# Sums of exp(phi) from a block of ones in the key products, a reordered plan, and 74 unread matmuls in the head

## The chip, the cores and the metric

The kernel runs on one core of a Trainium2 chip. The metric is the device time of one execution in microseconds. The core has a matrix engine (TensorE, PE in the profile; its weight loads are PEld), a vector engine (VectorE, DVE), a scalar engine (ScalarE, ACT), a general engine that here mostly issues loads (GpSimd, POOL) and a queue that issues stores (SyncE, SP). Sixteen DMA engines move data between HBM and the core's memory (SBUF); matmul results go to eight banks of a second memory (PSUM).

## The reference

Attention through 32 memory slots for 8 batches and 8 heads, then a channel mix over the joined heads. Shapes: q, k, v are 8 x 8 x 576 x 64, phi is 8 x 8 x 576 x 32; the weights w_k, w_v, w_r are 512 x 1024, 1024 x 512 and 512 x 512.

```
a = exp(phi - max);  a = a / (sum a + 1e-09)        # max and sum over the 576 tokens
k_m = einsum('bhsm,bhsd->bhmd', a, k);  v_m likewise from v
scores = q @ k_m.T / 8;  attn = softmax(scores)
x = attn @ v_m, heads joined to 512 columns
x_prev = x moved down by one token
xk = mu_k*x + (1-mu_k)*x_prev;  xr = mu_r*x + (1-mu_r)*x_prev
out = sigmoid(xr @ w_r) * (relu(xk @ w_k)**2 @ w_v)
```

What the kernel computes stands to this as follows: it takes exp(phi) without the maximum, multiplies it with k and v, and divides the products afterwards by a sum of exp(phi). The sum runs over the tokens for each head and slot, as the products do; the tile `rz` holds its reciprocal, one column for each of two groups of heads.

## The kernel before

**Tiles.** A token of a batch stands on a partition: the 576 tokens of a head are 64 partitions with nine tokens each (NJ = 9), and 128 partitions hold two heads' worth; four pairs (HH = 4) make a batch. `kvs` are two tiles (one for even, one for odd batches) with room for k and v; `qs` and `ems` (exp(phi) in bf16) are doubled likewise. The channel mix works in c blocks of tokens: block c0 is batch 0 (576 tokens, in halves a of 320 and b of 256 columns), c1 to c8 follow at 512 tokens (448 for the last).

**Order.** There is no loop that sets the order. `PLAN` is a list of words, and the program issues each word's instructions in that order; each engine then runs its own instructions strictly in that order. `BANKS` lists which PSUM bank each new product takes. A word is `batch:step`, `p:load`, `c<block>:<eighth>`, `g:<tile>` or `o:<tile>`.

**Steps of attention** (batch in front of the colon): `exp` (ScalarE, L252) makes exp(phi), `exp0` and `exp1` half of it. `k`, `v`, `kv` (L264) are the products of exp(phi) with k, v or both: 72 matmuls, weights 64 x 32, 64 columns for each of k and v; `k0c` and `k1c` do one half of the rows. `z` (L273) is nine matmuls of exp(phi) with a two-column tile of ones, and a reciprocal on VectorE (L276). `nk` and `ak` (VectorE or ScalarE, L287 for the latter) scale k by it into `kbd`; `nv`, `av` scale v. `tk`, `ta` transpose `kbd` (L321) and copy it (VectorE or ScalarE, L326). `q0`, `q1` turn q on VectorE (L339). `s`, `s0`, `s1` are the scores (32 matmuls, L354) and their exp on ScalarE (L359). The sum over slots and its spreading goes over VectorE (`fe`, `fs`, `fo`, or in smaller parts `qe`, `qs`, `qo`: L386, L396, L398, L405) or, in batch 0, over TensorE and ScalarE for one half (`l0`, `l1`: L369, L374; `h0z`, `h1z`: L379). `y0` to `y3` weigh (L414, tile `atn`). `x0m`, `x1m` are attn @ v_m (L308) and casts on VectorE and ScalarE (L426). `d0d`, `d2d` difference to the previous token (L438), `k0d`, `k0e`, `r0d` and so on mix (L449 to L452) into `xkT` and `xrT`.

**Batch 0** has a shorter way: `nk0`, `nk1`, `nr0`, `nr1` scale v_m by the sums and the mix factors (VectorE, L460, tile `vm`, which reads `mu_m`), and `mk0`, `mk1`, `mr0`, `mr1` (L308, casts L477) give the mixed halves at once. `mub` (L218, with `sel`) makes `mu_m`, `mu` the factors `mu1`.

**Channel mix.** `c1:5` is an eighth of the hidden columns for block 1: four matmuls (L560), relu on ScalarE (L564), square on VectorE (L572), or on ScalarE if the word ends in s (L570). `g:7` is the gate of a 128-token tile (four matmuls L593, tanh L596). `o:7` is its output: eight matmuls (L610), one VectorE instruction (L612) and the store; `o:0a`, `o:0b` are halves of the columns.

**Unread matmuls.** `0:busy4x4` issues four matmuls of a tile of zeros with 4 x 128 columns into a bank that nothing reads (L211).

**Loads.** `p:` words and two before the plan (`PRE`: half of k for batch 0, the identity) are issued on POOL in plan order, except phi of batch 0 (ScalarE's queue) and the mix factors (SP's). In the trace POOL issues a load when the one eight places earlier has landed, or when its buffer is free.

Of the kernel before, what the change touches and what calls it, by code (L numbers as in the profile page):

```python
# [46 lines left out]
    "01234567012345670123407516234075163240567132045671324671035246710352467103254671032546713205467130254671"  # L47
    "30254617302517302465710243657102436571024635170246351760351724603571260547312643712643710524637105247610"
    "5324761053621053612536012534760125346710254736102574631025746310257463102574631025746310257463102574"
# [3 lines left out]
NJ = 9  # L53
# [6 lines left out]
def kernel(  # L60
# [44 lines left out]
    kvs = [const.tile([128, 2, HH, NJ, D], BF16, name=f"kv{i}") for i in range(2)]  # L105
# [16 lines left out]
    def load_rows(dst, src):  # L122
        nc.gpsimd.dma_start(out=dst.rearrange("p h j d -> p h (j d)"), in_=rows(src))  # L123
# [7 lines left out]
    def load_batch(b):  # L131
        for what in LOADS.get(b, LOADS[None]):
            if what == "phi":
                load_phi(b, nc.gpsimd)
            elif what == "q":
                load_q(b)
            else:
                load_rows(kvs[b % 2][:, "kv".index(what)], (k, v)["kv".index(what)][b])

    load_phi(0, nc.scalar)  # L140
    nc.vector.memset(zeros, 0.0)
    mu2 = const.tile([2 * ND, 128], F32, name="mu2")
# [13 lines left out]
    def preload(word):  # L156
# [8 lines left out]
        else:  # L165
# [3 lines left out]
            else:  # L169
                dst = qs[n % 2].rearrange("p (h j) d -> p h j d", j=NJ) if what == "q" else kvs[n % 2][:, "kv".index(what)]  # L170
# [20 lines left out]
    sel = const.tile([2 * ND, 2 * HH, M], F32, name="sel")  # L191
# [7 lines left out]
    mu_m = const.tile([128, 2, 2, 2, D], F32, name="mu_m")  # L199
# [35 lines left out]
    def attention(b):  # L235
# [13 lines left out]
        kv5, em = kvs[b % 2], ems[b % 2]  # L249
# [4 lines left out]
        def ekv(parts, cs=(0, 1)):  # L254

            def go():
                w = parts.stop - parts.start
                kvps = {c: ps_tile([128, w, D], F32, "kvps") for c in cs}
                for i in range(w):
                    st.setdefault("kv"[parts.start + i], {}).update({c: kvps[c][:, i, :] for c in cs})  # L260
# [410 lines left out]
```

## Time and profile before

| | us |
|---|---|
| three timed runs | 203.2, 203.49, 205.34 (median 203.49) |
| the profiled execution | 202.35 |
| its span in the trace | 200.3 |
| its mean granted TensorE clock | 0.996 of full speed |

Rows of a timeline read: start in us, duration in us, engine, line, operation, output<-inputs, shapes, count; the bracket is how long the engine was idle before and what it waited for. Rows that the view has merged give the time from the first start to the last end; the time from one row's start to the next one's is what a step cost its engine. A matmul's row holds its latency too, so two neighbouring rows overlap. The page's columns by stretches give busy us and, in brackets, the count of instructions.

### The profile page before, as it was taken

The numbers are of one execution on the slowest core, as the hardware profiler recorded it, in microseconds if no ns is written. First come the engines' busy times: TensorE is split into PE (matmuls) and PEld (weight loads), VectorE is DVE, ScalarE is ACT, GpSimd is POOL, SyncE is SP. The second block draws the span as 40 slices with busy tenths as digits, with TensorE's granted clock in tenths as the row PEclk, the third lists the DMA queues.
The fourth block names the chain that finished last, engine by engine and source line by source line (L and its number), as shares of the span: only waits on it lengthen the run. The fifth ranks groups of instructions, "written<-read, shape, count | busy, mean of one in ns | idle before, by whom it ended". The sixth has DMA issues, their size and how long they took to land.

```text
span 200.3 us, 5430 instructions
## 1 busy us (share of the span) xinstructions
PE 187.6 (94%) x2186; PEld 98.3 (49%) x2186; DVE 149.3 (75%) x383; ACT 145.3 (73%) x313; POOL 29.8 (15%) x45
## 2 busy tenths in 40 slices
PE   1678999998999999999999999999999999999992
PEld 1355764764554445544456644444444444444451
DVE  2348579999889999999799989999769941132232
ACT  2337999568787899799899987996598679761300
POOL 7843232202123002050300000000000000000000
PEclk9999999999999999999999999999999999999998
DMA  6999999999999999999999202502170060022455
GB/s 161 194 265 209 206 207 253 210 225 289 240 206 285 293 255 202 266 161 271 229 226 218 57 23 65 126 0 56 40 171 2 3 157 0 0 52 55 105 123 139
DMA packets 24522, 31.29 MB, mean 156 GB/s; under 512 B 1961, under 2 KB 19633, under 8 KB 24497
## 3 DMA queue, kind: packets, MB, share of 16 engines
q0 software_dynamic: 17392, 20.91, 55.9%
q1 hardware_dynamic: 6336, 9.18, 17.9%
q10 hardware_dynamic: 768, 0.85, 1.4%
q8 instruction: 17, 0.28, 0.5%
q14 instruction: 9, 0.07, 0.1%
HBM read 38.28 MB, written 9.44 MB: 238 GB/s over the span
## 4 chain that ended last, share of the span: by engine, by line
PE 77%; DMA 17%; POOL 2%; ACT 1%; DVE 1%; issue 1%; POOLq 0%
PE pk L560 29%; PE pv L610 28%; PE pr L593 14%; DMA kv<-in_v_dram 11%; DMA ph<-in_phi_dram 5%; PE kvps L264 3%; PE nops L308 2%; PE scps L354 1%; POOL q L178 1%; POOL kv L126 1%; PE zps L273 1%; ACT em L252 1%; PE mxps L308 1%; DVE atn L414 0%; POOL kv L123 0%
## 5 line engine op out<-in xcount | busy, mean ns | idle before, releaser
L560 PE MATMUL pk<-xkT,wk 128*128 128x512 bf16 (+4 forms) x352 | 68.1, 341 | 0.2 <-ACT xkT L477 0.2
L610 PE MATMUL pv<-wv,sq 128*128 128x512 bf16 (+1 forms) x328 | 66.1, 353 | 0.0
L564 ACT ACTIVATE rl<-pk 128x512 bf16<-128x512 f32 (+3 forms) x80 | 43.5, 553 | 9.9 <-PE pk L560 9.1
L560 PEld LDWEIGHTS <-wk 128*128 128x128 bf16 x352 | 32.8, 98 | 28.7 <-issue 1.0
L610 PEld LDWEIGHTS <-sq 128*128 128x128 bf16 x328 | 31.5, 98 | 29.8 <-issue 0.2
L612 DVE SCALAR_TENSOR_TENSOR o<-sg,pv 128x512 f32<-128x512 f32 (+1 forms) x41 | 24.7, 612 | 15.7 <-PE pv L610 15.2
L593 PE MATMUL pr<-wr,xrT 128*128 128x512 bf16 x144 | 36.1, 380 | 0.2 <-DVE eT L386 0.2
L596 ACT ACTIVATE sg<-pr 128x512 f32<-128x512 f32 x36 | 21.0, 596 | 9.8 <-PE pr L593 9.7
L572 DVE TENSOR_TENSOR sq<-rl 128x320 bf16<-128x320 bf16 (+5 forms) x55 | 16.5, 326 | 15.5 <-ACT rl L564 15.2
L570 ACT ACTIVATE sq<-rl 128x512 bf16<-128x512 bf16 (+5 forms) x49 | 23.7, 504 | 1.2
L449 ACT ACTIVATE mu_d<-diff,mu 128x576 bf16<-128x576 bf16 x26 | 18.7, 774 | 3.8 <-DVE diff L439 2.2
L593 PEld LDWEIGHTS <-xrT 128*128 128x128 bf16 x144 | 13.3, 98 | 15.8 <-issue 0.7
L339 DVE STREAM_TRANSPOSE qT<-q 128x576 uint32<-128x576 uint32 x16 | 11.9, 760 | 4.2 <-DMA q<-in_q_dram 4.2
L426 ACT CAST x<-nops 128x320 bf16<-128x320 f32 (+1 forms) x34 | 11.7, 409 | 4.7 <-PE nops L308 4.6
L414 DVE TENSOR_TENSOR atn<-e,lz 128x256 bf16<-128x256 bf16 (+2 forms) x30 | 12.9, 462 | 0.4 <-ACT lz L379 0.3
L359 ACT ACTIVATE e<-scps 128x288 bf16<-128x288 f32 x32 | 10.5, 416 | 3.5 <-PE scps L354 3.3
L438 DVE TENSOR_TENSOR diff<-x 128x512 bf16<-128x512 bf16 (+1 forms) x42 | 12.3, 349 | 0.6 <-ACT x L426 0.5
L264 PE MATMUL kvps<-kv,em 64*32 64x64 bf16 (+1 forms) x792 | 9.7, 214 | 2.6 <-DMA kv<-in_v_dram 2.0
L264 PEld LDWEIGHTS <-em 64*32 64x32 bf16 x792 | 8.0, 94 | 7.2 <-issue 4.6
L405 DVE STREAM_TRANSPOSE lz<-se 128x576 f32<-128x576 f32 (+3 forms) x17 | 11.4, 686 | 0.0
L452 DVE TENSOR_TENSOR xkT<-x,mu_d 128x1152 bf16<-128x1152 bf16 x14 | 10.4, 752 | 1.4 <-ACT mu_d L449 1.1
L252 ACT ACTIVATE em<-ph 128x1152 bf16<-128x1152 f32 (+1 forms) x9 | 9.3, 1049 | 2.9 <-DMA ph<-in_phi_dram 2.9
(65 smaller groups left out, 147.7 us busy)
## 6 DMA issues: line engine op xcount, KB each, us to landing
out_dram<-o SPq DMA_DIRECT2D x61, 128.0 KB, 2.4
kv<-in_v_dram POOLq DMA_DIRECT2D x8, 576.0 KB, 18.4
ph<-in_phi_dram POOLq DMA_DIRECT2D x7, 576.0 KB, 14.8
kv<-in_k_dram POOLq DMA_DIRECT2D x7, 576.0 KB, 16.8
q<-in_q_dram POOLq DMA_DIRECT2D x6, 576.0 KB, 14.0
q<-in_q_dram POOLq DMA_DIRECT2D x4, 288.0 KB, 12.2
out_dram<-o SPq DMA_DIRECT2D x18, 64.0 KB, 6.1
wk<-in_moe_w_k_dram POOLq DMA_DIRECT2D x2, 512.0 KB, 13.7
```

Source lines behind the costliest of these rows:

```text
L264: nc.tensor.matmul(kvps[c][g * M:(g + 1) * M], lhsT=em[ROWS[c], j, g, :], rhs=kv5[ROWS[c], parts, g, j, :], start=j == 0, stop=j == NJ - 1 ...
L414: nc.vector.tensor_mul(st["at"][:, c, sl], st["e"][:, c, sl], st["lz"][:, c, sl])
L438: nc.vector.tensor_sub(d[:, :, lo:hi], x[:, :, lo:hi], x[:, :, p0:p0 + hi - lo])
L449: nc.scalar.activation(t[:, i], st["d"][:, pr + i, :], AF.Copy, scale=mu1[:, o:o + 1])
L560: nc.tensor.matmul(pk[:, p0 - lo:p1 - lo], lhsT=wk_sb[:, di, fi * 128:(fi + 1) * 128], rhs=xk_T[:, di, p0 % RING:p0 % RING + p1 - p0], sta ...
L564: nc.scalar.activation(rl, pk, AF.Relu, scale=HALF_ROOT)
L570: nc.scalar.activation(sq[:, fi, p:p + p1 - p0], rl[:, part], AF.Square)
L572: nc.vector.tensor_mul(sq[:, fi, p:p + p1 - p0], rl[:, part], rl[:, part])
L593: nc.tensor.matmul(pr, lhsT=xr_T[:, di, c0:c0 + 128], rhs=wr_sb[:, di, :], start=(di == 0), stop=(di == ND - 1))
L596: nc.scalar.activation(gated[t], pr, AF.Tanh, scale=0.5)
L610: nc.tensor.matmul(pv[:, cols], lhsT=sq[:, fi, p:p + 128], rhs=wv_sb[:, fi, cols], start=(fi == 0), stop=(fi == NF - 1))
L612: nc.vector.scalar_tensor_tensor(o[:, cols], in0=gated[t][:, cols], scalar=1.0, in1=pv[:, cols], op0=AL.add, op1=AL.mult)
```

## The change

- `kvs` becomes one tile with five blocks: k of even and odd batches, a block of ones written once by a memset, v of odd and even batches. The steps `ko` and `kov` are the products with k and ones, or k, ones and v: as many matmuls as `k` and `kv`, with 128 and 192 columns in place of 64 and 128. Every column of the ones' product holds the sum, and `zk` (or `zk0`, `zk1` for one half) takes its first column's reciprocal for each half: two VectorE instructions. Batches 1 to 7 use them and have no `z` step; batch 0 keeps `z`, now between `k0c` and `k1c`.
- `sel` and `mu_m` take the memory of two later work tiles (the fourth of `sg` and of `o`).
- The unread matmuls become 23 of 512 columns, 16 of 384, 25 of 128 and 10 of 256 (74), in place of 4, 3, 7, 1 and 12 (27).
- `PLAN` and `BANKS` are written anew throughout. At the head: `k:0b` is loaded before `q:00`, phi of batch 1 before v of batch 0, the columns 4-8 of wk before 0-4; `mub` moves behind `q1`; batch 1's `exp` moves ahead of `l0`; `mk0` and `mk1` both stand ahead of the first block of c0, and `mr0`, `mr1` come later.

```
 PLAN = [
-    "p:q:00 0:mub 0:mu 0:exp1 0:exp0 0:z 0:q0 0:busy4x4 p:k:0b 0:k0c 0:k1c 0:busy3x1 p:q:01 0:ak p:v:0 0:q1 0:busy7x1",
-    "0:tk 0:s1 0:s0 0:v 0:fe1 0:fs1 p:phi:1 0:nr0 0:l1 0:nk0 0:nr1 0:fo1 0:busy1x1 p:wk:0-4 0:l0 0:nk1 1:exp",
-    "0:busy12x2 0:h1z 0:y3 0:y2 0:y1 0:h0z 0:y0 0:mk1 p:wk:4-8 0:mk0 c0:2b c0:0as c0:0bs 0:mr0 c0:7b c0:5a 1:z c0:7a",
-    "c0:6bs c0:4b p:k:1 1:k p:q:10 1:ak 1:q0 c0:2a p:q:11 1:q1 0:mr1 c0:4a 1:ta c0:6a c0:5b 1:s1 1:s0 1:fe1 1:qe0",
-    "1:fs1 c0:1bs 1:qe1 p:wr:0-4 c0:3bs p:v:1 1:fo1 c0:3a g:1 1:fs0 1:qo0 1:y0 g:3 1:y2 g:0 1:qo1 1:y3 1:v 1:av",
-    "p:wv:2-4 1:y1 g:2 c0:1a 1:x0m o:3b o:0b 1:x1m 1:d0d 1:d2d p:phi:2 1:k0d 2:exp o:2b p:wv:0-2 1:k2e p:k:2 o:1b 2:z",
-    "o:1a o:0a 1:r2d o:3a c1:7s c1:0 2:k p:q:2 2:q1 2:ak 2:q0 c1:2 c1:6 1:r0d 2:ta c1:1s o:2a 2:s 2:fe0 2:fs0 2:qe2",
-    "2:qe3 p:v:2 2:v 2:av c1:4s 2:fs1 c1:3 2:fo0 2:fo1 p:phi:3 2:y3 p:k:3 g:5 2:y0 c1:5s 2:y1 3:exp g:4 2:y2 p:v:3",
...
+    "0:busy23x4 0:exp0 0:exp1 0:k0c 0:z p:k:0b p:q:00 p:q:01 0:k1c 0:busy16x3 0:ak 0:ta 0:q0 0:q1 0:mub 0:s1 0:s0",
+    "0:qe2 0:qe3 p:phi:1 p:v:0 0:busy25x1 0:fs1 0:qo2 0:qo3 1:exp 0:l0 0:v 0:h0z 0:y2 0:y3 0:l1 0:y0 0:nk0 0:nk1",
+    "0:busy10x2 0:h1z 0:y1 p:wk:4-8 0:nr1 0:mk0 0:mk1 c0:6a c0:7b p:wk:0-4 c0:5bs c0:7a c0:3bs p:k:1 0:nr0 c0:1b",
+    "c0:3a c0:2a c0:4b p:q:10 0:mr0 1:ko p:q:11 1:zk 1:nk c0:4a 1:q0 c0:6bs 1:q1 c0:1a 0:mu 1:ta 0:mr1 c0:0a 1:s0",
+    "1:s1 1:qe1 p:wr:0-4 1:qe0 1:fe1 c0:0bs p:v:1 c0:5as 1:fs0 c0:2bs 1:fs1 g:2 1:qo0 1:fo1 g:3 g:0 1:v 1:y0 1:qo1",
+    "1:y2 1:nv 1:y1 g:1 1:y3 1:x0m p:wv:0-2 1:x1m 1:d0d o:3a 1:d2d 1:k0d o:2a p:wv:2-4 o:1a 1:k2e o:0a o:3b o:1b",
+    "1:r0d p:phi:2 2:exp p:k:2 o:0b o:2b c1:3s 2:ko p:q:2 2:zk 2:ak 1:r2d c1:4s c1:6s 2:tk 2:q0 g:7 2:q1 c1:0 p:v:2",
+    "c1:5 2:s 2:qe2 2:qe3 2:qe1 2:fs1 2:qe0 2:fs0 2:qo2 2:y2 c1:7s g:6 2:fo0 2:v 2:qo3 p:phi:3 2:y0 c1:1s c1:2s g:5",
...
-    kvs = [const.tile([128, 2, HH, NJ, D], BF16, name=f"kv{i}") for i in range(2)]
+    kvs = const.tile([128, 5, HH, NJ, D], BF16, name="kvs")
+    KV = ((0, 2, 4), (1, 2, 3))
...
+    nc.vector.memset(kvs[:, 2].rearrange("p h j d -> p (h j d)"), 1.0)
...
         def ekv(parts, cs=(0, 1)):
             def go():
-                w = parts.stop - parts.start
-                kvps = {c: ps_tile([128, w, D], F32, "kvps") for c in cs}
...
+                which = "k1v"[parts]
+                at = KV[b % 2][parts]
+                at = slice(at[0], at[-1] + 1, at[1] - at[0] if len(at) > 1 else 1)
+                kvps = {c: ps_tile([128, len(which), D], F32, "kvps") for c in cs}
...
-                                             rhs=kv5[ROWS[c], parts, g, j, :],
+                                             rhs=kvs[ROWS[c], at, g, j, :],
...
+        def recip_sum(cs=(0, 1)):
+            def go():
+                if "rz" not in st:
+                    st["rz"] = own([128, 2], F32, "rz", 3)
+                for c in cs:
+                    nc.vector.reciprocal(st["rz"][:, c:c + 1], st["1"][c][:, 0:1])
+            return go
...
-    mu_m = const.tile([128, 2, 2, 2, D], F32, name="mu_m")
+    mu_m = work.tile([128, 2, 2, 2, D], F32, name="mu_m", tag="o3")
```

In the rest of the plan the three first `kov` steps with what follows them read `3:kov p:q:3 3:zk 2:d2d 2:d0d 3:ak 3:q1 3:av o:7 2:k2e 3:tk`, `4:kov 3:x0m 4:zk 3:d0d 4:ak`, and `5:kov p:q:5 5:zk 3:r2e 4:s`; batch 7's comes ahead of batch 6's, as `7:kv` and `6:kv` do before. The last words of both plans are `o:34 o:35`.

More of the change, by code (lines that the diff above doesn't have):

```diff
@@ L169, in preload @@
             else:
-                dst = qs[n % 2].rearrange("p (h j) d -> p h j d", j=NJ) if what == "q" else kvs[n % 2][:, "kv".index(what)]
+                dst = qs[n % 2].rearrange("p (h j) d -> p h j d", j=NJ) if what == "q" else kvs[:, KV[n % 2]["k1v".index(what)]]
                 src = {"q": q, "k": k, "v": v}[what][n]
@@ L189 @@
         nc.vector.memset(ones[ROWS[hg], hg:hg + 1], 1.0)
-    sel = const.tile([2 * ND, 2 * HH, M], F32, name="sel")
+    sel = work.tile([2 * ND, 2 * HH, M], F32, name="sel", tag="sg3")
     nc.vector.tensor_copy(sel, identity[:2 * ND, :2 * HH].unsqueeze(2).to_broadcast([2 * ND, 2 * HH, M]))
@@ L248, in attention @@
         x0 = b * S % RING
[L249 removed]
+        em = ems[b % 2]
         def exp_phi(hs=slice(0, None)):
@@ L256, in go @@
             def go():
-                w = parts.stop - parts.start
-                kvps = {c: ps_tile([128, w, D], F32, "kvps") for c in cs}
-                for i in range(w):
-                    st.setdefault("kv"[parts.start + i], {}).update({c: kvps[c][:, i, :] for c in cs})
+                which = "k1v"[parts]
+                at = KV[b % 2][parts]
+                at = slice(at[0], at[-1] + 1, at[1] - at[0] if len(at) > 1 else 1)
+                kvps = {c: ps_tile([128, len(which), D], F32, "kvps") for c in cs}
+                for i, what in enumerate(which):
+                    st.setdefault(what, {}).update({c: kvps[c][:, i, :] for c in cs})
                 for j in range(NJ):
@@ L480, in attention @@
         two = [(0, 0), (0, 1), (1, 0), (1, 1)]
-        steps = {"exp": exp_phi, "kv": ekv(slice(0, 2)), "k": ekv(slice(0, 1)), "v": ekv(slice(1, 2)),
-                 "z": esum, "nk": norm_k(), "nv": norm_v(), "ak": norm_k(by_act=True), "av": norm_v(True), "tk": tr_k(), "s": scores((0, 1)), "load": reload,
+        steps = {"exp": exp_phi, "kv": ekv(slice(0, 3, 2)), "k": ekv(slice(0, 1)), "v": ekv(slice(2, 3)),
+                 "kov": ekv(slice(0, 3)), "ko": ekv(slice(0, 2)), "z": esum, "zk": recip_sum(), "nk": norm_k(), "nv": norm_v(), "ak": norm_k(by_act=True), "av": norm_v(True), "tk": tr_k(), "s": scores((0, 1)), "load": reload,
                  "mu": load_mu, "mub": load_mu_b}
@@ L494, in attention @@
             steps[f"k{i}c"] = ekv(slice(0, 1), (i,))
-            steps[f"v{i}c"] = ekv(slice(1, 2), (i,))
+            steps[f"ko{i}c"] = ekv(slice(0, 2), (i,))
+            steps[f"zk{i}"] = recip_sum((i,))
+            steps[f"v{i}c"] = ekv(slice(2, 3), (i,))
             steps[f"exp{i}"] = lambda i=i: exp_phi(slice(2 * i, 2 * i + 2))
```

8 lines of the change are left out of this document (4 added, 4 removed), and 29 rows, old and new, of the table PLAN.

## The prediction

> **What bounds the kernel now.** I read the page's busy shares, then the engines' busy time by stretches, and the chain that ended last; the timelines by engine follow where a part needs them.
>
> ```profile
> span 200.3 us, 5430 instructions
> ...
> PE 187.6 (94%) x2186; PEld 98.3 (49%) x2186; DVE 149.3 (75%) x383; ACT 145.3 (73%) x313; POOL 29.8 (15%) x45
> ```
> ```profile
> 50.00:80.00 30.00, 30.00 (x425) 15.10 (x424) 28.03 (x69) 25.57 (x55) 5.22 (x7) 1.00 1.17 247
> ```
> ```profile
> 5.31 10.93 DMA ph<-in_phi_dram
> ...
> 27.71 22.24 DMA kv<-in_v_dram
> 49.99 0.88 PE kvps L264 x72
> ...
> 57.88 0.20 PE zps L273 x9
> ...
> 196.46 0.02 issue
> ```
>
> The columns after the stretch are PE, PEld, DVE, ACT and POOL. From 50 to 80 us TensorE is busy all 30.00 us, and the chain runs on TensorE from 49.99 to its last matmul at 196.46, so there every removed matmul microsecond is a microsecond of the result. Before that the chain goes through two loads: phi of batch 1 until 16.24, and v of batch 2, which lands at 27.71 + 22.24 = 49.95. So the kernel is bound by the loads up to 50 us and by TensorE's own work behind it. VectorE is nearly full too (28.03 of 30).
>
> **The seven sums that leave.** Batches 1 to 7 lose the step z: nine 128-row products into 2 columns. The chain gives 0.20 us for one (57.88). 7 x 0.20 = 1.40 us less on TensorE. Batch 0 keeps its z.
>
> **The wider products.** In its place k (batches 1, 2) goes from 64 to 128 columns and kv (batches 3 to 7) from 128 to 192. What a step costs is start to next start:
>
> ```profile
> 24.46 0.75 PE L264 MATMUL kvps<-kv,em 64*32 64x64 bf16 x72
> 25.15 0.72 PE L560 MATMUL pk<-xkT,wk 128*128 128x320 bf16 x4
> ...
> 44.05 0.90 PE L264 MATMUL kvps<-kv,em 64*32 64x64 bf16 x72
> 44.89 1.90 PE L560 MATMUL pk<-xkT,wk 128*128 128x512 bf16 x8
> ```
> ```profile
> 66.90 7.07 PE L560 MATMUL pk<-xkT,wk 128*128 128x512 bf16 x32
> 73.81 1.89 PE L593 MATMUL pr<-wr,xrT 128*128 128x512 bf16 x8
> ...
> 79.25 0.90 PE L264 MATMUL kvps<-kv,em 64*32 64x128 bf16 x72
> 80.08 1.90 PE L610 MATMUL pv<-wv,sq 128*128 128x512 bf16 x8
> ...
> 83.75 0.81 PE L264 MATMUL kvps<-kv,em 64*32 64x128 bf16 x72
> 84.48 0.47 PE L354 MATMUL scps<-qT,kmT 32*32 32x288 bf16 x32
> ```
>
> 64 columns: 0.69 and 0.84 us; 128 columns: 0.83 and 0.73. Doubling the columns cost nothing that these show, 72 matmuls at about 10 ns each, so the step goes by count of instructions, not by columns. For k I take +0.03 each, 0.06 together (from zero to 0.14). 192 columns is in no row. Streaming bounds it: 512 columns take 6.91/32 = 0.216 us, so 192 take 0.081. The 72 are nine rounds over eight tiles (four heads, two row halves), so one tile streams at least 9 x 0.081 = 0.73 us, and a step at 128 columns spends about 0.1 of its 0.73 to 0.83 on entering and leaving. So a kov step takes at least some 0.83 against the mean 0.78 of the two rows, +0.05. The upper end supposes that a tile takes its next weights only after its product ended, as the rounds at 128 columns allow: of 0.73 - 0.10 = 0.63 us each ninth is 0.070, of which 0.054 streams, leaving 0.016 to add; if all that and as much again is exposed, 9 x (0.081 + 0.032) + 0.1 = 1.12, +0.34. I take +0.12, nearest the 128-column rows: 5 x 0.12 = 0.60 (0.25 to 1.70). So sums and products together save 1.40 - 0.06 - 0.60 = 0.74 us.
>
> The Trainium skill's page "TensorE: Matmul & The Clock Gate", Part 3 (Packing small matmuls), speaks against this part: it puts a pack of tiles at one product's duration plus about 4 ns for each further tile. By that, an estimate, nine rounds of eight at 192 columns are 9 x (81 + 28) = 0.98 us, 1.08 with entry, and the saving shrinks to 1.40 - 0.06 - 1.50 = -0.16 us; the same rule gives 0.59 for 64 columns, where the trace has 0.69 at least, and 0.83 for 128, where it has 0.73 and 0.83, so it is neither confirmed nor refuted here.
>
> **The wait for v of batch 2.**
>
> ```profile
> 48.57 0.48 PE L354 MATMUL scps<-qT,kmT 32*32 32x288 bf16 x32
> 49.99 0.88 PE L264 MATMUL kvps<-kv,em 64*32 64x64 bf16 x72 [0.94 <-DMA kv<-in_v_dram]
> ```
>
> In both plans v of batch 2 is the nineteenth load of POOL's queue, behind the same bytes, so it still lands at 49.95. In the new order TensorE does c1's blocks 3, 4, 5 and gates 6 and 7 ahead of 2:v, and no longer c1's blocks 1 and 2, nor two z. That is three more steps of four 512-column matmuls (0.86 each) less 0.40: 2.2 us more work. TensorE comes to 2:v at 49.05 + 2.2 = 51.2, when v has landed. The wait of 0.94 us goes, and it isn't replaced unless the head gains over 1.3 us.
>
> **The loads in POOL's queue.** k:0b passes q:00, phi:1 passes v:0, the second half of wk the first, and wv's halves both stand ahead of phi:2. SP's queue has only stores, in the order of the o steps; the store traffic ahead of 50 us is the same eight half tiles. Each place in the queue lands about when the load in that place lands now:
>
> ```profile
> 13.89 0.81 PE L264 MATMUL kvps<-kv,em 64*32 64x64 bf16 x72 [1.09 <-DMA kv<-in_v_dram]
> ...
> 16.26 1.16 ACT L252 ACTIVATE em<-ph 128x1152 bf16<-128x1152 f32 x1 [0.38 <-DMA ph<-in_phi_dram]
> ...
> 21.90 0.88 POOL L162 DMA_DIRECT2D wv<-in_moe_w_v_dram  x1 [1.95 <-DMA wk<-in_moe_w_k_dram]
> ```
> ```profile
> 32.93 0.64 PEld L264 LDWEIGHTS <-em 64*32 64x32 bf16 x72 [0.42 <-DMA kv<-in_v_dram]
> ```
>
> So phi:1 comes at 13.9 instead of 16.2, v:0 at 16.2 instead of 13.9, and the later half of wk at about 21.7. The last two bound the new head.
>
> **The head: 74 unread matmuls, and the reordered steps.**
>
> ```profile
> 0.82 0.11 DVE L141 MEMSET zeros<- 128x64 uint32 x1 [0.82 <-PEq L655]
> ...
> 2.61 0.16 DVE L185 CAST identf<-identity 8x8 f32<-8x8 bf16 x1 [1.67 <-POOL identity masks.py:199]
> ...
> 4.11 1.19 PE L218 MATMUL mub<-mu,sel 8*128 8x128 f32 x4 [4.11 <-DMA mu<-in_moe_mu_r_dram]
> ...
> 6.56 1.87 PE L211 MATMUL idle<-zeros 128*128 128x512 bf16 x4
> ...
> 12.07 0.74 PE L354 MATMUL scps<-qT,kmT 32*32 32x288 bf16 x32 [0.39 <-DVE kmT L326]
> ...
> 15.20 2.74 PE L211 MATMUL idle<-zeros 128*128 128x256 bf16 x12
> ...
> 17.77 0.85 DVE L414 TENSOR_TENSOR atn<-e,lz 128x256 bf16<-128x256 bf16 x2 [0.31 <-ACT lz L379]
> 18.25 1.01 PE L308 MATMUL mxps<-atn,vm 32*64 32x256 bf16 x40 [0.31 <-DVE atn L414]
> ...
> 19.45 1.95 PE L560 MATMUL pk<-xkT,wk 128*128 128x256 bf16 x12 [0.19 <-ACT xkT L477]
> ```
> ```profile
> 20.80 0.60 PE L560 MATMUL pk<-xkT,wk 128*128 128x256 bf16 x4
> ```
>
> The new memset of ones is 18 times the one of zeros (0.11 us): at most 2.0 us on VectorE, which there waits 1.67 us for the identity anyway, and the 0.3 left over delays constants that are used much later. Nothing.
>
> The unread matmuls of now run at half speed: four of 512 columns in 1.87 us, and twelve of 256 in 2.74 is 0.21 each, where 0.108 is full speed by the 512-column row. At 20.80 four of 256 take 0.60 with one's latency of 0.27 in it, 0.11 each: full speed. (The granted clock's column says 1.00 throughout and doesn't show this.) TensorE had then been at work almost without gap since 13.89; so the release came 4.0 to 6.9 us after work set in. In the new head work sets in at 0.93, right behind the zeros: 9 to 16 of the first 23 cost 0.43 us, the rest 0.216, and they end at 7.9 to 9.4; I take 8.6. Then k0c, z and k1c, 0.9 us at full speed (their operands, the first and second load, are in by then), 9.5. Then 16 of 384 columns, 2.6 us, 12.1. Then the turned k, and mub's four matmuls (1.19 now, 0.6 to 1.2), which stand ahead of the scores: these start at about 13.1, 1.0 us later than now. All 39 + 35 unread matmuls otherwise fill waits of TensorE.
>
> From the scores' start to mk the chain is now 18.25 - 12.07 = 6.18 us and runs on VectorE. In it are a wait of 0.31 for lz (phi:1's exp held up ScalarE; it now runs earlier), two products for nr (0.31 each by the row below) and the fourth atn (0.43), which in the new order are not ahead of mk0; folding in parts adds four instruction starts, some 0.2. 6.18 - 0.31 - 0.62 - 0.43 + 0.2 = 5.0, so mk0 at 18.1.
>
> ```profile
> 16.41 0.31 DVE L460 SCALAR_TENSOR_TENSOR vm<-kvps,rz,mu_m 128x128 bf16<-128x128 f32 x1
> ...
> 19.06 1.55 DVE L477 CAST xkT<-mxps 128x256 bf16<-128x256 f32 x4 [0.44 <-PE mxps L308]
> ...
> 21.74 1.15 PE L560 MATMUL pk<-xkT,wk 128*128 128x256 bf16 x8
> ```
>
> v:0 at 16.2 plus its product (0.7) and two vm (0.6) is 17.5, just hidden behind it; without that cover it costs nothing until it passes 18.1. Now the casts of xkT end 20.61 - 18.25 = 2.36 us after mk begins; plus nr1 on VectorE (0.31) gives 20.8. Key 7b ends there, 5bs (0.43) and 7a (0.54) at 21.9 to 22.0; and 3bs needs the later half of wk, 21.7. At 21.74 the present kernel has done three half blocks and mr0 (0.54 + 2 x 0.43 = 1.40 us, and 0.4 to 0.6 for mr0's 24 by the row of 40), the new one has done four (1.94) by 22.0. Net 0.1 to 0.2 later: +0.2. Bounds: -0.33, because 1:v can't start ahead of 32.93 and stands 0.33 us deeper in the new list (a block 1a and gate 2 in, gate 1 and a z out); and +1.2, from the late end of the release plus a slow mub. The page just named, Part 1, puts the release at about 3.4 us of sustained work; by that estimate the 23 end at 7.6 and the head reaches the bound of -0.33.
>
> **Waits added.** zk stands on VectorE behind the casts and squares queued there and ahead of the next turn of q; kbd on ScalarE (or VectorE) waits for it, and tk or ta on TensorE for that. Price of cover lost: see the third rival. Two one-column reciprocals in place of one two-column instruction (0.164) add some 0.14 x 7 = 1.0 us to VectorE, inside the 2.0 us that it idles in each 30; uncovered it is 1.0.
>
> ```profile
> 39.38 0.38 PE L273 MATMUL zps<-ones,em 128*128 128x2 bf16 x9
> ```
> ```profile
> 24.18 0.17 DVE L276 RECIPROCAL rz<-zps 128x2 f32<-128x2 f32 x1
> ...
> 42.79 0.16 DVE L276 RECIPROCAL rz<-zps 128x2 f32<-128x2 f32 x1
> ```
>
> **Sum.** -1.40 + 0.06 + 0.60 - 0.94 + 0.2 = -1.48 us. The end behind the last matmul stays. The profiled execution took 202.35 us (span 200.3 and 2.05 around it), so 200.9; the three timed runs have a median of 203.49, 1.14 above that execution, so on their scale 202.0.
>
> **Rivals.** *Wide products stream-bound*: kov at 1.08, +0.30 each where I took +0.12, 0.9 more: 202.9. For it: nothing shows 192 columns; against: no slope from 64 to 128. *Early head and free columns*: head -0.33 and kov +0.05 each: 1.40 - 0.06 - 0.25 + 0.94 + 0.33 = 2.36 less, 201.1. For it: the release at its early end. *VectorE's queue takes over* (slower): z's matmuls ended at 23.1 and 39.6, their reciprocals ran at 24.2 and 42.8, 1.1 and 3.2 us behind, which cost nothing as k came later. Now the lag stands between k and its transposition. Between ko and ta or tk TensorE has 1.51 us (batch 1) and 1.73 (batch 2), of which reciprocals and kbd (2 x 0.38) take 1.06; with lags of now the stalls are 0.65 and 2.5: 202.0 + 3.2 = 205.2. It decides from stalls over 1.5 us in all. Against it: the new order puts only some 0.5 us of casts, folds and o's more ahead of 2:zk than TensorE's eight o halves take. *Cold head* (slower): the release doesn't come from zeros. Then the 23 end at 10.8, k and z take 1.7, the 16 take 5.1, mub 1.2, and scores start near 19.1, 6 us after mine: 208. Against it: the release of now came after mostly such matmuls.
>
> **Numbers.** Forecast 0.42, stream-bound 0.14, early head 0.17, VectorE's queue 0.20, cold head 0.07. One per cent, about what a measurement here can tell from no change, is 201.46 and 205.52. Faster: the early head and a third of the forecast's spread, 0.30. Slower: cold head, over half of the queue case and small tails, 0.22. Same: 0.48. Range 200.3 to 205.3: below 201.1 for the run-to-run offset of the profiled execution, above to the queue case; the cold head and the far part of the queue case are left out.
>
> **What would show it.** The step's start-to-start at 192 columns (0.83 to 1.12); no wait of TensorE for v at 50 us; first key near 19.3 and 3bs near 22; zk within 0.6 us of its product in batches 1 and 2. I am wrong if TensorE has new waits ahead of ta, tk or the scores in the middle, or if the 16 unread matmuls run at 0.32 us.

## The result, and the profile after

The changed kernel takes 201.35 us (median of 20 runs, 200.59 to 202.99), the kernel before 203.28 (median of 20, 202.29 to 205.34). The ratio of their times is 0.9909, with a 95% interval of 0.989 to 0.9928: 0.9% faster, some 1.9 us, where 1.48 was forecast. Medians in this document are of all runs of a kernel; the ratios leave out single runs that lie more than 1.5% above the fastest of the same kernel.

The two profiled executions are much closer to each other: 201.65 us after, 202.35 before. The profiled execution of before was 0.93 us faster than that kernel's median, and the one of after 0.30 slower than its own; so the profiles can show 0.70 us of the 1.93 and no more. That gap has to be kept in mind in all that follows.

Of the 0.70, only 0.4 lie within the span (200.3 against 199.9 us). The rest is the time around it: 2.05 us in the profiled execution of before, 1.75 in that of the changed kernel. This holds in all runs: the changed kernel and the seven kernels of the experiments below that are built from its program spend 1.73 to 1.85 us outside of their span, the kernel before and the five built from its program 1.81 to 2.17, on average 1.8 and 2.0. So some 0.2 us of the 1.9 have nothing to do with the order of the work. What makes them is not shown.

From the page of the changed kernel, and the last step of its chain of waits:

```profile
span 199.9 us, 5381 instructions
...
PE 191.9 (96%) x2148; PEld 99.6 (50%) x2170; DVE 151.3 (76%) x401; ACT 144.5 (72%) x311; POOL 29.7 (15%) x45
```
```profile
196.05 0.42 DVE o L628
```

The last VectorE instruction starts at 196.05 instead of 196.49, so TensorE's work ends about 0.4 us earlier. TensorE's busy time went up by 4.3 us although the sums left, because the unread matmuls went from 6.2 to 13.6 us: busy time says nothing here about time gained.

The head, from its timeline (start, duration, engine, line, operation; in the bracket the idle time before it and what it waited for):

```profile
0.99 8.01 PE L214 MATMUL idle<-zeros 128*128 128x512 bf16 x23 [0.99 <-DVE zeros L143]
...
1.36 1.98 DVE L144 MEMSET kvs<- 128x2304 bf16 x1 [0.43 <-issue]
...
13.45 0.50 PE L368 MATMUL scps<-qT,kmT 32*32 32x288 bf16 x32
13.88 1.57 PE L214 MATMUL idle<-zeros 128*128 128x128 bf16 x25
...
18.63 1.11 PE L322 MATMUL mxps<-atn,vm 32*64 32x320 bf16 x27 [0.71 <-DVE vm L474]
...
19.97 0.41 PE L322 MATMUL mxps<-atn,vm 32*64 32x256 bf16 x13 [0.23 <-ACT xkT L491]
...
20.32 4.58 PE L576 MATMUL pk<-xkT,wk 128*128 128x320 bf16 x36
```

The first 23 unread matmuls end at 9.0, where 8.6 was reckoned, and those of 128 columns behind the scores already run at 0.06 us each, full speed. The scores start at 13.45 (13.1 reckoned) and mk at 18.63 (18.1), released by VectorE as forecast. The first key starts at 20.32, not at 19.3, so it is 1.69 us behind the start of mk, where before it was 1.20 (18.25 to 19.45). Both mk steps stand ahead of the first key in both plans; now mk1 waits 0.23 us until casts of mk0 have freed a PSUM bank.

The products with the block of ones, and the first place where v of batch 2 is used, from TensorE's timeline:

```profile
45.46 0.80 PE L269 MATMUL kvps<-kvs,em 64*32 64x128 bf16 x72
46.20 1.90 PE L576 MATMUL pk<-xkT,wk 128*128 128x512 bf16 x7
...
52.97 0.75 PE L269 MATMUL kvps<-kvs,em 64*32 64x64 bf16 x72
...
60.42 0.94 PE L269 MATMUL kvps<-kvs,em 64*32 64x192 bf16 x72
61.29 1.90 PE L626 MATMUL pv<-wv,sq 128*128 128x512 bf16 x7
...
85.23 0.94 PE L269 MATMUL kvps<-kvs,em 64*32 64x192 bf16 x72
86.09 0.55 PE L368 MATMUL scps<-qT,kmT 32*32 32x288 bf16 x32
```

From start to next start 128 columns cost 0.74 us and 192 columns 0.87 and 0.86. The product with v of batch 2 has no bracket: it no longer waits. But it starts at 52.97, where 51.2 was reckoned. What held TensorE up shows in the timeline between 29 and 38 us:

```profile
29.68 0.49 PE L368 MATMUL scps<-qT,kmT 32*32 32x288 bf16 x27 [0.37 <-issue]
...
33.79 1.28 ACT L612 ACT_TABLE_LOAD   x1
...
34.90 1.04 PE L609 MATMUL pr<-wr,xrT 128*128 128x512 bf16 x3
35.09 2.06 ACT L612 ACTIVATE sg<-pr 128x512 f32<-128x512 f32 x4
...
36.20 0.82 PE L322 MATMUL nops<-atn,vb 32*64 32x320 bf16 x11 [0.27 <-ACT sg L612]
...
37.20 0.31 PE L322 MATMUL nops<-atn,vb 32*64 32x256 bf16 x5 [0.18 <-ACT sg L612]
37.52 0.71 PE L626 MATMUL pv<-wv,sq 128*128 128x256 bf16 x5
```

Four gates' tanh (`sg`) wait on ScalarE behind a table load of 1.28 us, and x0m and x1m wait for those `sg`. The kernel before has the same load, and its x steps don't wait there:

```profile
31.61 1.28 ACT L596 ACT_TABLE_LOAD   x1
```

Now the load starts 2.2 us later on ScalarE, behind an exp of the scores that starts 1.6 us later (30.15 against 28.51) and one square more, while TensorE comes to x0m only 1.1 us later than before. The gate that starts at 34.90 ends its four matmuls at 34.90 + 4 x 0.216 = 35.77; from there to 37.52 pass 1.75 us, in which two x steps cost 0.27 + 0.25 elsewhere in the trace. So 1.2 us went there, and 0.37 at the scores of batch 1.

### The profile page after: what moved, and what is told of

Its sections match the earlier page's. It is cut to its first block, busy times and chain, and to the rows that moved or that the text cites. A ratio compares the mean times of both kernels' runs of the same rounds, so it can differ in the third digit from the quotient of the medians.

```text
span 199.9 us, 5381 instructions
## 1 busy us (share of the span) xinstructions
PE 191.9 (96%) x2148; PEld 99.6 (50%) x2170; DVE 151.3 (76%) x401; ACT 144.5 (72%) x311; POOL 29.7 (15%) x45
## 4 chain that ended last, share of the span: by engine, by line
PE 91%; ACT 4%; DVE 2%; issue 1%
PE pv L626 32%; PE pk L576 31%; PE pr L609 14%; PE idle L214 5%; PE kvps L269 4%; PE scps L368 2%; PE nops L322 2%; ACT sg L612 1%; PE mxps L322 1%; ACT e L373 1%; ACT L612 1%; DVE atn L428 1%; ACT rl L580 1%; PE ktps L335 1%; DVE lz L419 0%
## 5 line engine op out<-in xcount | busy, mean ns | idle before, releaser
L576 PE MATMUL pk<-xkT,wk 128*128 128x512 bf16 (+4 forms) x344 | 67.2, 340 | 0.4
L580 ACT ACTIVATE rl<-pk 128x512 bf16<-128x512 f32 (+3 forms) x80 | 42.5, 552 | 13.1 <-PE pk L576 12.0
L612 ACT ACTIVATE sg<-pr 128x512 f32<-128x512 f32 x36 | 20.9, 594 | 13.6 <-PE pr L609 13.5
L588 DVE TENSOR_TENSOR sq<-rl 128x320 bf16<-128x320 bf16 (+5 forms) x55 | 15.8, 323 | 14.6 <-ACT rl L580 14.0
L586 ACT ACTIVATE sq<-rl 128x512 bf16<-128x512 bf16 (+5 forms) x49 | 24.5, 518 | 1.3
L463 ACT ACTIVATE mu_d<-diff,mu 128x576 bf16<-128x576 bf16 x30 | 21.4, 768 | 3.9 <-DVE diff L453 3.4
L214 PE MATMUL idle<-zeros 128*128 128x512 bf16 (+3 forms) x74 | 13.6, 346 | 1.0 <-DVE zeros L143 1.0
L466 DVE TENSOR_TENSOR xrT<-x,mu_d 128x1152 bf16<-128x1152 bf16 x14 | 10.5, 751 | 3.5 <-ACT mu_d L463 3.2
L428 DVE TENSOR_TENSOR atn<-e,lz 128x320 bf16<-128x320 bf16 (+2 forms) x31 | 12.9, 452 | 0.1
L419 DVE STREAM_TRANSPOSE lz<-se 128x320 f32<-128x320 f32 (+3 forms) x21 | 11.9, 587 | 0.1
L410 DVE TENSOR_REDUCE se<-eT 128x18 f32<-128x576 bf16 (+3 forms) x15 | 10.9, 729 | 0.2
```

What stands on the lines that cost most here:

```text
L214: nc.tensor.matmul(ps.rearrange("p (a b) -> p a b", b=128), lhsT=zeros, rhs=zeros.unsqueeze(1).to_broadcast([128, blocks, 128]), start=Tru ...
L428: nc.vector.tensor_mul(st["at"][:, c, sl], st["e"][:, c, sl], st["lz"][:, c, sl])
L463: nc.scalar.activation(t[:, i], st["d"][:, pr + i, :], AF.Copy, scale=mu1[:, o:o + 1])
L576: nc.tensor.matmul(pk[:, p0 - lo:p1 - lo], lhsT=wk_sb[:, di, fi * 128:(fi + 1) * 128], rhs=xk_T[:, di, p0 % RING:p0 % RING + p1 - p0], sta ...
L580: nc.scalar.activation(rl, pk, AF.Relu, scale=HALF_ROOT)
L586: nc.scalar.activation(sq[:, fi, p:p + p1 - p0], rl[:, part], AF.Square)
```

## The experiments

Each kernel ran beside the kernel before on the same chip; ratios are to that kernel, with 95% intervals. One per cent is 2.03 us. Edits of `PLAN` are given as words; the PSUM banks go with their steps.

**1. The old order with an early start of TensorE's work** (theory 1: the unread matmuls bring the gain).

```
+0:busy23x4                    (first word)
-0:busy3x1   +0:busy16x3
```

> The kernel before with only its unread matmuls changed: 23 of 512 columns as the first work of TensorE, and 16 of 384 in place of 3 of 128 behind k1c; its order and its sums stay. Theory 1 (the measured gain of 1.9 us is more than the 0.4 us between the ends of TensorE's work in the two profiles because in most runs of the kernel before TensorE's clock is released later than in its profiled one, after the first keys have begun, and the early unread matmuls end that): 1.0 to 1.8 us faster than before, and the spread of its runs narrower than before's 3 us. Theory 2 (the gain is the seven sums, 0.74 us net, and the wait for v of batch 2, 0.94; the unread matmuls only fill waits): within 0.3 us of before.

Measured: 204.68 us, ratio 1.0046 (1.0016 to 1.0076), slower. From its TensorE timeline:

```profile
14.59 0.51 PE L353 MATMUL scps<-qT,kmT 32*32 32x288 bf16 x32 [0.38 <-DVE kmT L325]
...
20.14 0.99 PE L307 MATMUL mxps<-atn,vm 32*64 32x256 bf16 x40 [1.46 <-DVE atn L413]
```

The scores start 2.5 us later than in the first profile of before, behind the sixteen unread matmuls, and mk 1.9 us later. The edit added a delay of its own, so it speaks neither for nor against the clock. Experiment 7 tries to do without that delay.

**2. The new order with the old unread matmuls.**

```
-0:busy23x4 +0:busy4x4   -0:busy16x3 +0:busy3x1   -0:busy25x1 +0:busy8x1   -0:busy10x2 +0:busy12x2
```

> The changed kernel with the 27 unread matmuls of before (4 of 512 columns, 3 of 128, 8 of 128, 12 of 256) in place of the 74; everything else stays. Theory 1: 1.0 to 2 us slower than the changed kernel, that is 0 to 0.9 us faster than before, with first keys that run at half speed in part (0.27 us for 320 columns in place of 0.135) in the profile or a wide spread. Theory 2: as the changed kernel, 1.6 to 2.2 us faster than before.

Measured: 201.85 us, 0.9933 (0.9906 to 0.996). The new order gains 0.67% without the additional unread matmuls; with them it was 0.91%. The difference, 0.24% or 0.5 us, has overlapping intervals: between the two theories, and not settled by the time. Its profile lacks the sign that theory 1 named: the first 36 key matmuls take 4.58 us, as in the changed kernel, so they run at full speed. Most of the gain does without the additional matmuls.

**3. The new order with the sums as a step of their own again, ahead of k.**

```
-1:ko ... 1:zk   +1:z 1:k      -3:kov ... 3:zk   +3:z 3:kv      (batches 1 to 7)
```

> The changed kernel with the step z back in batches 1 to 7, directly ahead of the k products, which go back to 64 and 128 columns; no block of ones is read. Both theories: 0.9 us slower than the changed kernel by the rows of its profile (7 sums of 0.20 us less 5 times the 0.10 us by which a product with 192 columns is longer than one with 128, and no difference between 64 and 128), that is 1.0 us faster than before. Rival: less than 0.3 us slower, if TensorE's time at those places was covered by waits for loads or for VectorE.

Measured: 212.98 us, 1.0425 (1.0369 to 1.0481): some 9 us slower than before. The list of TensorE's waits names why:

```profile
PE kvps L268 <- DVE rz L280: 7.7, 7, 2.2
```

In all seven batches the k product waited for the reciprocal of the sum just ahead of it, 1.1 us on average. The product doesn't read the reciprocal, so only the bank can be the cause: each z had the bank that k takes next, and it is free only when VectorE has read it. The kernel doesn't measure the sums' own price. What it does measure is how late VectorE is with a reciprocal in this order: up to 2.2 us.

**4. The old order with the block of ones.**

```
-1:z ... 1:k   +1:ko 1:zk      -3:z 3:kv   +3:kov 3:zk      (batches 1 to 7)
```

> The plan and the unread matmuls of before with the sums of batches 1 to 7 from the block of ones: ko or kov in place of k or kv, zk directly behind, no z. Theory 1 and 2 alike: 0.9 us less of TensorE's work, of which the part ahead of the wait for v of batch 2 (two sums, 0.4 us) lengthens that wait, so 0.5 us faster than before. Rival (VectorE's queue takes over): slower than before, with TensorE waiting for kbd ahead of ta or tk, most in batch 2, where the reciprocal ran 3.2 us behind its sum.

Measured: 203.21 us, 0.9985 (0.996 to 1.001): 0.3 us less, not clear of nothing. From its TensorE timeline:

```profile
50.27 0.89 PE L267 MATMUL kvps<-kvs,em 64*32 64x64 bf16 x72 [1.13 <-DMA kvs<-in_v_dram]
...
86.02 0.34 PE L267 MATMUL kvps<-kvs,em 64*32 64x192 bf16 x9 [1.19 <-issue]
```

The wait for v of batch 2 is 1.13 us (0.94 before), as the expectation had it grow, and within the product of batch 5 TensorE now stands for 1.19 us. The sums alone are worth little in the old order: the median span of its runs is 201.45 us, and so is that of the kernel before beside it, so the 0.3 us are the time around the span.

**5. Is it the load for batch 7?** In the profile of experiment 1 TensorE had waited 1.90 us for k of batch 7.

```
-p:phi:6 c3:2 7:kv 4:x1m 4:d0d c3:7 g:14   +p:phi:6 c3:2 4:x1m 4:d0d c3:7 g:14 7:kv
```

> The kernel before with one step moved: 7:kv, and nothing else, four words later, behind c3:7 and g:14, so that the loads of k and v of batch 7 have two more TensorE steps (1.73 us) in which to land. Theory 3 (in the profiled execution of before these loads landed just in time, but in its usual run TensorE waits 0.5 to 2 us for them, as it did for 1.90 us in the profile of the kernel with the warm head; the changed plan comes to 7:kov 12.0 us after issuing the first of the two where before it was 11.2): 0.5 to 1.2 us faster than before in the median, with no change of TensorE's work. Rival: within 0.2 us of before.

Measured: 203.5 us, 1.0002 (0.998 to 1.0025). Theory 3 falls: the gain that it names is outside of the interval.

**6. The term for v of batch 2 alone.**

```
-2:v 2:av c1:4s 2:fs1 c1:3   +c1:4s 2:fs1 c1:3 2:v 2:av
```

> The kernel before with 2:v and 2:av moved behind c1's blocks 4 and 3 (two TensorE steps, 1.73 us), so that TensorE comes to v of batch 2 after it has landed. The prediction's term: the wait of 0.94 us goes, 0.9 us faster than before. Rival: the time comes back as a wait further on (for v of batch 3, or for attention's steps of batch 2 that now come 0.9 us later in VectorE's and ScalarE's order), less than 0.3 us faster.

Measured: 202.8 us, 0.9983 (0.9963 to 1.0002): 0.35 us, not clear of nothing. The wait was gone at v of batch 2, and was back at the next load:

```profile
58.84 0.80 PE L263 MATMUL kvps<-kv,em 64*32 64x128 bf16 x72 [1.17 <-DMA kv<-in_v_dram]
```

This is v of batch 3. The rival was right, and its size nearly: here, taking a wait for one load away moved it to the next load, which lands no earlier.

**7. The clock in the old order, without a delay.** The later unread matmuls are doubled in number, so that they take as long at full speed as they did at half.

```
+0:busy23x4 (first word)   -0:busy4x4 +0:busy1x4   -0:busy3x1 +0:busy6x1   -0:busy7x1 +0:busy14x1
-0:busy1x1 +0:busy2x1   -0:busy12x2 +0:busy24x2
```

> The kernel before with 23 unread matmuls of 512 columns as TensorE's first work and the later unread ones doubled in number, since they run at twice the speed (1, 6, 14, 2 and 24 in place of 4, 3, 7, 1 and 12), so that no step waits longer behind them than now. Theory 1, mended (TensorE's clock is released late in the usual run of before): 0.5 to 1.5 us faster than before. Rival (the head is bound by loads, VectorE and ScalarE, and the clock was released before the first key in nearly all runs): within 0.3 us of before.

Measured: 206.21 us, 1.0148 (1.0113 to 1.0182), slower by 3 us. From its TensorE timeline, and then by stretches (the last three columns are granted clock, share of the DMA engines and GB/s):

```profile
10.77 0.55 PE L263 MATMUL kvps<-kv,em 64*32 64x64 bf16 x36 [1.54 <-DMA kv<-in_k_dram]
11.26 2.31 PE L210 MATMUL idle<-zeros 128*128 128x128 bf16 x20
```
```profile
10.00:12.50 2.50, 1.73 (x48) 1.64 (x48) 0.33 (x1) 0.37 (x1) 0.76 (x2) 0.69 1.20 201
12.50:15.00 2.50, 1.83 (x45) 1.22 (x42) 0.74 (x2) 0.24 (x1) 0.70 (x1) 0.63 1.13 318
```

The clock had been released (23 matmuls of 512 columns in 6.67 us), and then k1c waited 1.54 us for its load, third in the queue in this order; behind that the granted clock is 0.69 and 0.63, and the twenty unread matmuls take 0.11 us each, half speed, and now hold up the transposition of k. So this edit, too, added a delay of its own, and its time doesn't test theory 1. The profiles at hand do. In before's, the twelve first key matmuls take 1.95 us from 19.45, and in the five others with the same head (experiments 4, 5, 6, 10 and 11) 1.95 to 1.97. In experiment 10's the first four of them still run at about half speed (0.19 to 0.21 us for 256 columns, 0.108 later), and the twelve take 1.97. So a clock that is released behind the first key costs some 0.02 us there, and theory 1 needs 1 us or more.

The run also shows a use that the other three blocks of unread matmuls in the new order can have: they fill gaps in which the clock could be lost. That they are needed for it was not tried.

**8. The sums ahead of k, further ahead and in other banks** (new order).

```
-1:ko ... 1:zk   +1:z (3 to 5 TensorE steps or more) 1:k      (batches 1 to 7)
```

> The changed kernel with the step z back in batches 1 to 7, three to five TensorE steps ahead of the k products and in a PSUM bank that no step needs while its reciprocal is pending; k and kv go back to 64 and 128 columns. By the rows of the changed kernel's profile (seven sums of 0.20 less five products longer by 0.10) 0.9 us slower than the changed kernel, 1.0 us faster than before. Rival: no slower than the changed kernel, if the sums only moved TensorE's work into waits for loads.

Measured: 220.21 us, 1.0754 (1.0696 to 1.0813). TensorE's longest waits:

```profile
PE zps L277 <- ACT em L254: 6.8, 4, 3.5
PE zps L277 <- DVE vb L313: 3.6, 1, 3.6
```

Now TensorE comes to the sum before exp(phi) is made, and once to a bank that is still in use.

**9. The sums directly behind k** (new order).

```
-1:ko p:q:11 1:zk   +1:k 1:z p:q:11      -3:kov p:q:3 3:zk   +3:kv 3:z p:q:3      (batches 1 to 7)
```

> The changed kernel with z back in batches 1 to 7 directly behind the k products, where zk stood, so that TensorE waits neither for exp(phi) nor for a reciprocal; k and kv go back to 64 and 128 columns. If the sums as such are worth what the rows say (seven of 0.20 us less five products longer by 0.10): 0.9 us slower than the changed kernel, 1.0 faster than before, and no new wait of TensorE over 0.5 us. Rival (the place of the sum matters more than its time): 2 us or more slower than the changed kernel, with waits for kbd or for a PSUM bank.

Measured: 206.3 us, 1.0155 (1.0107 to 1.0203): 2.5% above the changed kernel's ratio, 5 us where the sums' own time gives 0.9. The waits:

```profile
PE zps L277 <- ACT x L439: 1.8, 4, 0.8
PE zps L277 <- DVE o L627: 1.2, 1, 1.2
```

Six of the seven z steps wait, these five for 3.0 us, for a bank that a cast or an output instruction still reads; the sixth waits 0.5 us. With the sums' own 0.9 us that makes 4.4 of the 5 us. The rival was right. Three placings of z in the new order failed for three reasons: the bank of the next step, exp(phi) not made, and no bank free. They were placed by a simple rule; a good place may exist and wasn't found. What is shown is that in these three placings a sum with a bank of its own, or with the next step's, costs far more in waits than its own time, while the sum that shares k's bank has no wait at its product. What the sums as such are worth in the new order is not measured by any of the three.

**10. Two products moved in the old order.** As in experiment 6, and 3:kv too.

```
-2:v 2:av c1:4s 2:fs1 c1:3   +c1:4s 2:fs1 c1:3 2:v 2:av
-3:kv 2:x1m g:6              +2:x1m g:6 3:kv
```

> The kernel before with 2:v and 2:av behind c1's blocks 4 and 3 (as tried alone) and also 3:kv behind 2:x1m and gate 6, so that neither wait for a load of v is left between 45 and 60 us. Theory 4 (up to 60 us before is bound by the landing of loads, the changed order isn't, and moving one product only moved the wait to the next load): 0.9 to 1.5 us faster than before, that is half or more of what the whole change gains. Rival: the 0.3 us of the single move stay, and the wait turns up behind a third load.

Measured: 202.65 us, 0.9947 (0.9921 to 0.9973): 1.1 us faster, over half of what the whole change gains. (Its interval and that of experiment 6 overlap a little.) Its profile has no wait of TensorE over 0.4 us behind 16 us. The chain that ended last by engines, first for before, then for this kernel:

```profile
PE 77%; DMA 17%; POOL 2%; ACT 1%; DVE 1%; issue 1%; POOLq 0%
```
```profile
PE 56%; DMA 35%; issue 4%; POOL 3%; DVE 0%; POOLq 0%
```

With two waits gone the chain goes through even more loads, the last of them k of batch 7:

```profile
97.39 0.80 PE L263 MATMUL kvps<-kv,em 64*32 64x128 bf16 x72 [0.25 <-DMA kv<-in_k_dram]
```

A wait of 0.25 us is enough to lead the chain there: its shares say which loads TensorE runs up against, not how long it stands. Nor can this profile show the gain. It is the slowest of the kernel's twelve runs (203.59), and its first key starts 0.86 us later than in the profile of before.

The gain has the size that theory 4 gave. That the old order runs at the pace of its loads past 50 us, and the changed one doesn't, can be read from the records of landings in the first two profiles. In the kernel before, v of batch 3 lands at 58.20 and its product starts at 58.34; k of batch 7 lands at 95.98 and its product starts at 96.11. In the changed kernel v of batch 2 lands at 49.33 and is used from 52.97, v of batch 3 at 58.38 and 60.42, v of batch 7 at 97.56 and 98.64. So v of batches 2 and 3 lands within 0.7 us of where it did, and the new order comes to its loads 1 to 3.6 us behind their landing. No load stands in the changed kernel's chain:

```profile
PE 91%; ACT 4%; DVE 2%; issue 1%
```

In the profiles of experiments 2 and 12, which have the same order, the chain goes through one load, v of batch 0, ahead of 17 us. So theory 4 holds for these profiles. The interval of the gain (0.5 to 1.6 us) leaves open how much of the 1.9 us this is.

**11. The same with the block of ones.** Edits of 10 and 4 together.

> The same, with the sums from the block of ones as well (as in the earlier run with the plan of before). Theory 4: the 0.9 us that this takes off TensorE now come through: 1.6 to 2.4 us faster than before, as the whole change. Rival: TensorE's waits for VectorE's late reciprocals in batches 4 and 5 (1.19 us in the earlier run) take half of it, 1.0 to 1.5 us faster than before.

Measured: 204.05 us, 1.0023 (0.9997 to 1.0049). Against experiment 10 the sums now cost 0.76%, 1.5 us, where 0.9 us of gain was expected; worse than the rival's figure too. Its chain and its timeline in batch 5:

```profile
PE 71%; DVE 10%; ACT 8%; DMA 5%; issue 2%; POOL 2%; POOLq 0%; DVEq 0%; ACTq 0%
```
```profile
84.08 1.14 PE L267 MATMUL kvps<-kvs,em 64*32 64x192 bf16 x72
...
88.14 0.23 DVE L287 RECIPROCAL rz<-kvps 128x1 f32<-128x1 f32 x2
88.34 0.62 ACT L299 ACTIVATE kbd<-kvps,rz 128x128 bf16<-128x128 f32 x2 [1.31 <-DVE rz L287]
89.89 0.28 PE L333 MATMUL ktps<-identity,kbd 128*128 128x128 bf16 x2
```

The loads have left the chain (5%) and VectorE and ScalarE have come in (18%). The reciprocal runs 3 us behind its product, ScalarE stands 1.31 us for it, and the transposition of k starts 1.75 us after it. This lag is what the prediction's third rival spoke of, in the old order. That it costs the 1.5 us is not shown: TensorE has no idle time at this transposition and none over 0.5 us behind 16 us, and the profiled execution (203.25) is the second fastest of its twelve, below the one of experiment 10. The 0.8 us by which the median lies over it are not explained by that profile.

**12. Fewer unread matmuls at the start of the changed kernel.**

```
-0:busy23x4   +0:busy18x4
```

> The changed kernel with 18 in place of 23 unread matmuls of 512 columns at the start. In the changed kernel's profile the 23 end at 9.0 us and hold up k0c, whose load and exp(phi) are in by 8.3, and the scores start 1.4 us later than before. With 18 they end at about 7.9: scores 1.0 us earlier and first key 0.5 to 1.0 us earlier. If the head still sets the end: 0.4 to 0.9 us faster than the changed kernel. Rival: the later half of wk and q of batch 1 hold the order back, no change.

Measured: 200.67 us, 0.9872 (0.9835 to 0.9909): the fastest kernel of the study, 0.37% below the changed kernel's ratio, with intervals that overlap a little. The size is what was expected, the way to it can't be seen:

```profile
0.99 6.92 PE L213 MATMUL idle<-zeros 128*128 128x512 bf16 x18 [0.99 <-DVE zeros L142]
...
16.91 0.75 PE L268 MATMUL kvps<-kvs,em 64*32 64x64 bf16 x72 [1.54 <-DMA kvs<-in_v_dram]
```

In this execution (201.57, the slowest of its six) v of batch 0 landed 1.05 us later than in the profile of the changed kernel, and the first key started at 20.36, as there. The scores start at 13.20, not 1.0 but 0.25 us earlier than there, because the product of k ahead of them now waits 0.69 us for its load. That the head comes earlier in its other runs is likely and not shown.

## Why the prediction was right

Its direction and its size hold: 1.48 us forecast, 1.9 measured. By its steps, against the two profiles:

| step | forecast us | in the profiles |
|---|---|---|
| seven sums gone | -1.40 | gone: 0.23 to 0.30 each from start to next start, -1.95 |
| k at 128 columns, two | +0.06 | 0.76 and 0.74 us against 0.69 and 0.84: 0 |
| kv at 192 columns, five | +0.60 | 0.876 on average against 0.776 for 128: +0.50 |
| wait for v of batch 2 | -0.94 | gone |
| head, to the fifth key | +0.2 | first four keys end at 20.32 + 1.94 = 22.26, not 22.0: +0.46 |
| new waits between 29 and 38 us | none | +1.6 |
| end of TensorE's work | -1.48 | 196.46 to 196.03: -0.43 |

The first row is a term that the prediction sized by another rule than its own. It took 0.20 us for a sum from the chain; by its rule, from a row's start to the next one's, the seven sums of the kernel before take 0.23, 0.24, 0.30, 0.30, 0.29, 0.30 and 0.29 us. Two of them:

```profile
57.72 0.37 PE L273 MATMUL zps<-ones,em 128*128 128x2 bf16 x9
58.02 0.34 PE L308 MATMUL nops<-atn,vb 32*64 32x320 bf16 x8
...
78.68 0.37 PE L273 MATMUL zps<-ones,em 128*128 128x2 bf16 x9
78.97 0.34 PE L308 MATMUL nops<-atn,vb 32*64 32x320 bf16 x8
```

The measured column then adds up to -0.33, where the trace has -0.43. So in this pair the forecast was some 1.05 us too good. The step that was missing is the 1.6 us around 29 to 38, made up in part by sums that were worth 0.55 us more than reckoned: the prediction asked what the sums' new place on VectorE would delay, and not what the new place of the first gates' tanh, with its table load, would delay on ScalarE. The 0.37 us of it ahead of the scores of batch 1 is also, though small, one of the signs that the prediction gave for being wrong.

In the runs the forecast was not too good but 0.45 us short, so that 1.48 and 1.9 lie so close is in part luck. Two things lie behind it. The prediction let the 2.05 us around the span stay, and they fell by 0.2 to 0.3. And it was made on an execution of before that is faster than that kernel's median by 0.93 us, while the changed kernel's profiled one is 0.30 slower than its own; the prediction had 1.14 us between the two scales and took it for an offset of both kernels.

What makes that execution fast is open. In its profile the scores start at 12.07 and the first key at 19.45. Five kernels whose plan is the same up to there (experiments 5, 6 and 10, and 4 and 11 but for the ones' memset) have the scores at 12.44, 12.78 and 13.22, and 12.95 and 13.04, and the first key at 19.77 to 20.31: the load of k:0b lands later there, and the rest of the old order's head comes later. A late head doesn't reach the end in every case, though. In experiment 5's profile the first key starts 0.32 us later and TensorE's work ends 0.14 us later (189.66 + 6.94), since the wait for v of batch 2 is shorter there by 0.23 us, among others; the execution takes 202.51 us. In experiment 6's, with its move, it is 0.42 and 0.45 us, and 202.70. So the later head alone makes up no more than a part of the 0.93 us. That the old order pays for each load that is late, and the changed one has room there, fits the landings under experiment 10; as the timed runs have no profiles, it is argued and not shown that this makes up the difference.

*The wait for v of batch 2*: right that it goes, and too simple in what it is worth. Alone it is worth 0.35 us, not clear of nothing (experiment 6), with the wait for v of batch 3 1.1 us (experiment 10). The change moves both: ahead of 3:kov stand 2:x1m, gates 6 and 8 and o:5 for o:4. The prediction counted the steps ahead of 2:v and stopped there.

*Sums*: the products were sized well and the sums too small, but they are no saving by themselves. In the old order the block of ones brings 0.3 us, not clear of nothing (experiment 4), and loses 1.5 us once the load waits are gone (experiment 11). In the new one its reciprocals run soon: 0.1 to 0.4 us behind the product in batches 1, 2 and 3, up to 1.5 in batch 5, where TensorE has work in between. That it therefore pays there is argued: no run has the new order without it and without waits for a bank or for exp(phi).

*Rivals*: the stream-bound product (1.08 us for 192 columns) is refuted by 0.87. The rule of the Trainium skill on "TensorE: Matmul & The Clock Gate", Part 3 (Packing small matmuls), from which that figure came, sees one pack; here nine packs follow each other and the measurement is a fifth below it. The cold head is refuted by the 25 unread matmuls in 1.57 us. The early head didn't come: in the changed kernel the release came some 5.8 us after work began, late in the 4.0 to 6.9 us that the prediction gave. VectorE's queue did not take over in the changed kernel; in experiment 11 it enters the chain.

*The unread matmuls*: called fillers of waits, worth nothing on their own; measured, they are worth 0.5 us in the new order with overlapping intervals (experiment 2), five fewer at the start do better by 0.37%, overlapping too (experiment 12), and in the old order they cost, by the delays that came with them (1 and 7).

## What to carry to other kernels

Before a wait for a load is counted as a gain, look at when the next loads in the queue land and what reaches them: moving one product gave 0.35 us, not clear of nothing, and moving two gave 1.1. A step that shortens one engine but puts a short instruction of a full engine into a chain has to be laid out together with that engine's queue; the same edit was worth -0.3 us, +1.5 and, in a plan made for it, an unmeasured part of -1.9. Size all terms of a sum by one rule: here the sums' 0.20 us came from another view than the products' times, and were 0.08 short each. And take the profiled execution's place among the timed runs seriously: here the one of before was 0.93 us faster than that kernel's median and the one of the changed kernel 0.30 slower than its own.

## What was not expected of the hardware

- The landing of the first loads moves the head: in six profiles with the same first steps the scores start anywhere from 12.07 to 13.22 us.
- The clock's release: the first 23 unread matmuls took 6.67 us (experiment 7), 7.46 (experiment 1) and 8.01 (changed kernel). With 0.427 us for a matmul at half speed and 0.216 at full speed, and 0.2 us of latency, that is a release some 3.0 to 5.8 us after work began. It can be lost again soon: in experiment 7 the granted clock was 0.63 to 0.69 behind a wait of 1.54 us.
- Matmuls of 64 x 32 weights cost the same with 64 and 128 columns (0.69 to 0.84 us for 72) and only 0.10 us more with 192.
- The memset of 2304 bf16 columns took 1.98 us, as long as the proportion to the small one (18 x 0.11) gives.
